# Mixing the last 64 tokens of two batches as two column tiles of the array

## Chip, cores, metric

The kernel runs on one core of one Trainium2 chip. The metric is the device time of one execution in microseconds (us). All runs quoted below were in the fast state (a program on one core has no second die to compare, so this rests on the spread of its own runs), and the granted TensorE clock of the profiled runs of before and after was 0.997 and 0.999. "Chunk" means 128 rows (tokens) of 512 values. PE is TensorE, DVE VectorE, ACT ScalarE, POOL GpSimd, SP SyncE, whose queue (SPq) starts most of the transfers that matter here.

## The reference

```python
# q, k, v: 8 batches x 8 heads x 576 tokens x 64;  x: 8 x 576 x 512
k_p = k.reshape(B, H, 72, 8, D).mean(axis=3)          # v_p likewise
attn = softmax(q @ k_p.T / 8)                         # 576 x 72 per head
x = (attn @ v_p).transpose(0, 2, 1, 3).reshape(B, S, H * D)
a1 = alpha1 * x + beta1
u = x + lam * np.einsum('ts,bsd->btd', w_tok, a1)     # token mix, 576 x 576
a2 = alpha2 * u + beta2
out = u + lam * (np.maximum(a2 @ w_ch1, 0.0) @ w_ch2) # 512 -> 2048 -> 512
```

576 tokens are four chunks of 128 and a remainder of 64. The remainders of two neighbouring batches share one chunk for everything after the token mix.

## The kernel before

The channel part runs in nine blocks of four chunks. Block n multiplies its chunks by both weight matrices and also prepares batch n+1: attention, token mix, transpose. A list of (place, function) pairs sets the order in which the pieces of a block are written into the program.

Every batch mixed its own five chunks, the fifth being the remainder. In `mix_T`, `c == 4` is the remainder; `xs` holds the scaled x of a batch, `wtT` the transposed weights. All 128 output rows were computed for it, and DVE read 64 of them: the upper half for an even batch, the lower half for an odd one.

```python
def att_AV(b, h):
    if "x" not in st:
        st["x"] = work.tile([P, 5, DM], FP, tag="x_tm", bufs=1, name="x_tm")
    ...
    nc.vector.tensor_tensor(out=x[:, :, dd:dd + D], in0=av[:, :, 0:64], in1=..., op=ALU.mult)

...
def mix_T(b, c, eng=nc.vector):
    key, s = chunk_of(b, c)                    # c == 4: the chunk (even b, 4), shared by two batches
    p0, p1 = (0, P) if c < 4 else (64 * (b % 2), 64 * (b % 2) + 64)
    xs = xs_pool[b % 2]
    ps_tok = gp("ps_tok")
    t0 = P * c - 64 * (b % 2) if c == 4 else P * c
    for sc in range(5):
        kk, at = (P, sc) if sc < 4 else (P, 5) if b % 2 else (65, 4)
        nc.tensor.matmul(out=ps_tok, lhsT=wtT[0:kk, at, t0:t0 + P],
                         rhs=xs[0:kk, sc, :], start=(sc == 0), stop=(sc == 4))
    nc.vector.tensor_tensor(out=s["u"][p0:p1, :], in0=st1[b]["x"][p0:p1, c, :],
                            in1=ps_tok[p0:p1, 0:DM], op=ALU.add)
    eng.tensor_tensor(out=s["u_bf"][p0:p1, :], in0=s["u"][p0:p1, :],
                      in1=al2_bc[p0:p1, :], op=ALU.mult)

def mix_uT(key):                               # u_bf -> u_fm, the operand of the channel part
    if key[0] > 1 or key == (0, 4):
        nc.sync.dma_start_transpose(out=u_fm[blk][...], in_=s["u_bf"])   # in SP's queue
        return
    ...                                        # otherwise a transpose on PE and a copy on ACT
```

SP's queue also carries the stores of results (`mlp_B`, when a chunk is finished) and the transposes of q for batch 2 (`att_F`, `att_Frem`). In the traces of before and after none of its 155 entries starts before the issue of the one ahead of it has ended, and an entry moved in the program moves in the queue (`rem_qT` from 85.36 to 77.51 us in the run with q first); this matters later.

The softmax here doesn't subtract the row's maximum and nothing guards it: scores larger than these inputs give would overflow.

## Time and profile before

| | before |
|---|---|
| time, 3 runs | 364.95 us (364.85 to 365.48) |
| span of the profiled run | 363.5 us |
| one matmul of 128 rows x 512 columns, in a dense stretch | 0.216 us |

The page and the stretches by stage are in the prediction. In the tiles' names, `ps_h` is the product of a block's chunks with `w_ch1`, `Hj` its maximum with 0 after a bias, made by ACT, `ps_ch` the product of `Hj` with `w_ch2`, `ps_tok` the token mix; `kpT` is the pooled k and `qT` and `rem_qT` the q of the attention, all transposed, `rem` standing for the last 64 tokens. What I compare later is the chain of waits in order of time: start, length, engine, tile and line, number of instructions. It is the best ruler for this kernel, because each piece on it starts when the one before allows it. First the group of the token mix (busy, mean ns of one, idle before and what ended it), then the chain. A matmul's record lasts 379 ns in the mean and the next starts 0.216 us after it, so the records overlap.

```profile
L518 PE MATMUL ps_tok<-xs,wtT 128*128 128x512 bf16 (+1 forms) x200 | 49.6, 379 | 1.8 <-DVE xs L484 1.8
```

```profile
65.44 1.25 PE ps_tok L518 x5
...
110.88 1.08 PE ps_tok L518 x5
...
118.01 4.32 PE ps_h L553 x20
...
155.06 4.32 PE ps_h L553 x20
...
303.26 13.81 PE ps_h L553 x64
```

The line at 110.88 is one of the four groups that the change takes out. 118.01, 155.06 and 303.26 are the first matmuls of blocks 2, 3 and 7. I use such starts as marks: the shift of a mark between two kernels is all that was won up to there.

### The profile page before, as it was taken

Reading aid. Unit: us, or ns where it says so; the run is one execution under the profiler, and the core shown is the slowest. Engines: PE = TensorE matmul, PEld = TensorE weight load, DVE = VectorE, ACT = ScalarE, POOL = GpSimd, SP = SyncE. Lnnn points to the kernel's source line nnn. Section 1 sums busy time; section 2 is a strip of 40 time slices with the busy share of each in tenths; the row PEclk is TensorE's granted clock in tenths of the full one; section 3 lists DMA queues with packets and bytes.
Section 4 is the critical chain, followed back from the end, with each engine's and each line's share of the span. In section 5 each row is a group of like instructions: output and inputs, shape, how many; then the busy total and the mean of one; then the engine's idle time right before and its main releaser. Section 6 shows DMA issues by size and latency. Waiting matters only on the chain.

```text
span 363.5 us, 5915 instructions
## 1 busy us (share of the span) xinstructions
PE 348.4 (96%) x2229; PEld 188.7 (52%) x2229; DVE 212.7 (59%) x456; ACT 153.9 (42%) x319; POOL 86.8 (24%) x99
## 2 busy tenths in 40 slices
PE   4888999899999999999999999999999999999994
PEld 1566666355644564456445644565456545545541
DVE  5574176669774878576857786677658761011011
ACT  2562995027800790069005910592049304703700
POOL 8469406252117000620053005300510000000000
PEclk9999999999999999999999999999999999999998
DMA  8999910998959872987198919872810032011012
GB/s 125 203 216 262 216 26 2 160 228 202 142 119 223 153 124 62 244 159 123 51 218 149 156 52 220 171 131 61 215 67 0 31 87 74 0 58 60 1 58 58
DMA packets 65886, 44.58 MB, mean 123 GB/s; under 512 B 32377, under 2 KB 57021, under 8 KB 65858
## 3 DMA queue, kind: packets, MB, share of 16 engines
q1 hardware_dynamic: 50480, 33.30, 38.3%
q0 software_dynamic: 15072, 10.76, 20.5%
q8 instruction: 17, 0.28, 0.3%
q10 hardware_dynamic: 306, 0.14, 0.2%
q14 instruction: 11, 0.09, 0.1%
HBM read 38.30 MB, written 9.44 MB: 131 GB/s over the span
## 4 chain that ended last, share of the span: by engine, by line
PE 90%; DVE 5%; ACT 1%; DMA 1%; issue 1%; ACTq 0%; DVEq 0%
PE ps_h L553 33%; PE ps_ch L571 33%; PE ps_tok L518 12%; PE ps_sc L450 4%; PE ps_av L469 2%; DVE x_tm L477 2%; PE ps_sc L453 1%; DMA vecs<-in_moe_alpha_dram 1%; PE ps_bc L278 1%; DVE kpT L416 1%; PE ps_kp L403 1%; DVE w L339 1%; PE ps_q L368 1%; DVE xs L484 0%; ACT u_fm L539 0%
## 5 line engine op out<-in xcount | busy, mean ns | idle before, releaser
L558 ACT ACTIVATE Hj<-ps_h,bias_cols 128x512 bf16<-128x512 f32 x144 | 98.7, 689 | 154.4 <-PE ps_h L553 153.5
L553 PE MATMUL ps_h<-u_fm,w 128*128 128x512 bf16 (+1 forms) x592 | 138.1, 374 | 1.3 <-ACT u_fm L539 1.1
L571 PE MATMUL ps_ch<-w,Hj 128*128 128x512 bf16 x576 | 134.2, 379 | 0.0
L571 PEld LDWEIGHTS <-Hj 128*128 128x128 bf16 x576 | 55.0, 98 | 62.0
L553 PEld LDWEIGHTS <-w 128*128 128x128 bf16 x592 | 63.4, 114 | 44.9 <-issue 1.8
L576 DVE TENSOR_TENSOR u_sb<-u_sb,ps_ch 128x512 f32<-128x512 f32 x36 | 24.7, 686 | 74.7 <-PE ps_ch L571 74.3
L518 PE MATMUL ps_tok<-xs,wtT 128*128 128x512 bf16 (+1 forms) x200 | 49.6, 379 | 1.8 <-DVE xs L484 1.8
L455 ACT ACTIVATE ET<-ps_sc 72x256 f16<-72x256 f32 (+1 forms) x128 | 44.5, 404 | 2.5 <-PE ps_sc L450 2.2
L520 DVE TENSOR_TENSOR u_sb<-x_tm,ps_tok 128x512 f32<-128x512 f32 (+1 forms) x40 | 27.5, 687 | 30.7 <-PE ps_tok L518 30.7
L477 DVE TENSOR_TENSOR x_tm<-ps_av,rec 128x320 f32<-128x320 f32 x64 | 31.4, 491 | 2.3
L147 POOL CAST rem_q<-rem_raw 128x256 bf16<-128x256 f32 x7 | 3.1, 437 | 123.3 <-DMA rem_raw<-in_q_dram 123.3
L518 PEld LDWEIGHTS <-wtT 128*128 128x128 bf16 (+1 forms) x200 | 19.2, 98 | 25.5 <-DVE xs L484 1.6
L522 DVE TENSOR_TENSOR u_bf<-u_sb,al_bc 128x512 bf16<-128x512 f32 (+1 forms) x38 | 29.0, 763 | 1.4
L438 DVE TENSOR_TENSOR v_u<-v_u 72x512 f32<-72x512 f32 (+1 forms) x48 | 28.3, 589 | 1.2
L450 PE MATMUL ps_sc<-qT,kpT 128*72 128x256 bf16 x128 | 25.4, 275 | 0.5 <-DVE kpT L416 0.4
L475 DVE RECIPROCAL rec<-ps_av 128x5 f32<-128x5 f32 x64 | 12.2, 191 | 18.6 <-PE ps_av L473 17.7
L469 PEld LDWEIGHTS <-ET 72*128 72x128 f16 x256 | 15.9, 98 | 11.9 <-issue 0.5
L162 POOL TENSOR_TENSOR k_raw<-k_raw 128x512 f32<-128x512 f32 x14 | 18.3, 1307 | 15.9 <-DMA k_raw<-in_k_dram 15.9
L164 POOL TENSOR_TENSOR k_bf<-k_raw 128x512 bf16<-128x512 f32 x14 | 19.4, 1386 | 1.1
L484 DVE TENSOR_TENSOR xs<-x_tm,lamal_bc 128x512 bf16<-128x512 f32 x26 | 18.3, 705 | 0.9
L469 PE MATMUL ps_av<-vp,ET 72*128 72x66 f16 x256 | 18.0, 193 | 0.3 <-ACT wtT L299 0.3
L416 DVE CAST kpT<-ps_kp 64x288 bf16<-64x288 f32 x26 | 11.8, 455 | 9.4 <-PE ps_kp L409 5.2
(111 smaller groups left out, 216.5 us busy)
## 6 DMA issues: line engine op xcount, KB each, us to landing
out_dram<-u_sb SPq DMA_DIRECT2D x32, 256.0 KB
k_raw<-in_k_dram SPq DMA_DIRECT2D x14, 512.0 KB
v_u<-in_v_dram SPq DMA_DIRECT2D x12, 512.0 KB
q_bf<-in_q_dram POOLq DMA_DIRECT2D x16, 256.0 KB, 6.7
w<-in_moe_w_ch_dram POOLq DMA_DIRECT2D x8, 512.0 KB, 10.9
v<-in_v_dram POOLq DMA_DIRECT2D x4, 256.0 KB, 6.8
out_dram<-u_sb SPq DMA_DIRECT2D x8, 128.0 KB
rem_raw<-in_q_dram SPq DMA_DIRECT2D x15, 64.0 KB
```

Source lines behind the costliest of these rows:

```text
L438: nc.vector.tensor_tensor(out=t[:, :, 0:n], in0=t[:, :, 0:n], in1=t[:, :, n:2 * n], op=ALU.add)
L450: nc.tensor.matmul(out=ps_sc[0:SPG, 0:256], lhsT=kpT_pool[u][:, half, h % 4, :], rhs=st["qT"][u][:, 2 * (h % 4):2 * (h % 4) + 2, :])
L455: nc.scalar.activation(out=ET[:, n0:n0 + n], in_=ps_sc[0:SPG, 0:n], func=AF.Exp, bias=0.0, scale=0.125)
L469: nc.tensor.matmul(out=av[:, c, :], lhsT=ET[:, m0:m0 + 128], rhs=vp1[:, hh, :])
L477: nc.vector.tensor_tensor(out=x[:, :, dd:dd + D], in0=av[:, :, 0:64], in1=rec.unsqueeze(2).to_broadcast((P, 5, D)), op=ALU.mult)
L518: nc.tensor.matmul(out=ps_tok, lhsT=wtT[0:kk, at, t0:t0 + P], rhs=xs[0:kk, sc, :], start=(sc == 0), stop=(sc == 4))
L520: nc.vector.tensor_tensor(out=s["u"][p0:p1, :], in0=st1[b]["x"][p0:p1, c, :], in1=ps_tok[p0:p1, 0:DM], op=ALU.add)
L522: eng.tensor_tensor(out=s["u_bf"][p0:p1, :], in0=s["u"][p0:p1, :], in1=al2_bc[p0:p1, :], op=ALU.mult)
L553: nc.tensor.matmul(out=ps_h[:, t0:t1], lhsT=w1_of(cc, j), rhs=u_fm[n][:, cc, t0:t1], start=(cc == 0), stop=(cc == 3))
L558: nc.scalar.activation(out=t, in_=ps_h, func=AF.Relu, bias=bias_cols[:, j:j + 1], scale=1.0)
L571: nc.tensor.matmul(out=ps, lhsT=Hj[n, j][:, 128 * m:128 * m + 128], rhs=w2[j // 4][:, j % 4, :], start=(j == 0), stop=(j == NJ - 1))
L576: nc.vector.tensor_tensor(out=u, in0=u, in1=ps, op=ALU.add)
```

## The change

The intent: the remainders of two batches, 64 output rows each, side by side in the array. In the trace after, such a matmul stands as a tile of 128*64, where one of 128 output rows stands as 128*128; in the built program the two of a pair sit at columns 0 and 64. The even batch's own mix goes away. The odd batch issues for each of the five accumulation steps one matmul for its partner into rows 0 to 63 of the accumulator and one for itself into rows 64 to 127. Since the partner's x must then live until the odd batch's mix, the two batches share a buffer of six sections: the even batch uses 1 to 5 with the remainder in 5, the odd one 0 to 4 with the remainder in 0. Sections 1 to 4 hold the full chunks of whichever batch came last.

```diff
 def att_AV(b, h):
-            st["x"] = work.tile([P, 5, DM], FP, tag="x_tm", bufs=1, name="x_tm")
+            st["x"] = st1[b - 1]["x"] if b % 2 else work.tile([P, 6, DM], FP, tag="x_tm", bufs=1, name="x_tm")
 ... (sections shifted by `odd` in the matmuls and in att_X)
-        nc.vector.tensor_tensor(out=x[:, :, dd:dd + D], in0=av[:, :, 0:64],
+        nc.vector.tensor_tensor(out=x[:, 1 - odd:6 - odd, dd:dd + D], in0=av[:, :, 0:64],
 def mix_T(b, c, eng=nc.vector):
-        p0, p1 = (0, P) if c < 4 else (64 * (b % 2), 64 * (b % 2) + 64)
+        parts = ((b % 2, 0, P),) if c < 4 else ((0, 0, 64), (1, 64, P))
         for sc in range(5):
-            ...
-            nc.tensor.matmul(out=ps_tok, lhsT=wtT[0:kk, at, t0:t0 + P],
-                             rhs=xs[0:kk, sc, :], start=(sc == 0), stop=(sc == 4))
+            for i, p0, p1 in parts:
+                kk, at = (P, sc) if sc < 4 else (P, 5) if i else (65, 4)
+                nc.tensor.matmul(out=ps_tok[p0:p1], lhsT=wtT[0:kk, at, P * c:P * c + p1 - p0],
+                                 rhs=xs_pool[i][0:kk, sc, :], start=(sc == 0), stop=(sc == 4))
+        for i, p0, p1 in parts:
+            ... (the add, once per part)
-        eng.tensor_tensor(out=s["u_bf"][p0:p1, :], in0=s["u"][p0:p1, :],
-                          in1=al2_bc[p0:p1, :], op=ALU.mult)
+        eng.tensor_tensor(out=s["u_bf"], in0=s["u"], in1=al2_bc, op=ALU.mult)
 # the order: mix_T(b, 4) only for odd b
-            todo.append((at, lambda c=c: mix_T(b, c)))
             if c < 4 or b % 2:
+                todo.append((at, lambda c=c: mix_T(b, c)))
-            todo.append((6.5, lambda: mix_T(0, 4)))          # block 0
```

More of the change, by code (lines that the diff above doesn't have):

```diff
@@ L466, in att_AV @@
         av = ps_av[:, 0:5 * 66].rearrange("p (c x) -> p c x", x=66)
+        odd = b % 2
         for c in range(4):
             m0 = 256 * (c % 2) + 128 * (c // 2)
-            nc.tensor.matmul(out=av[:, c, :], lhsT=ET[:, m0:m0 + 128],
+            nc.tensor.matmul(out=av[:, odd + c, :], lhsT=ET[:, m0:m0 + 128],
                              rhs=vp1[:, hh, :])
-        r0 = 512 - 64 * (b % 2)
-        nc.tensor.matmul(out=av[:, 4, :], lhsT=ET[:, r0:r0 + 128], rhs=vp1[:, hh, :])
+        r0 = 512 - 64 * odd
+        nc.tensor.matmul(out=av[:, 4 - 4 * odd, :], lhsT=ET[:, r0:r0 + 128], rhs=vp1[:, hh, :])
         rec = work.tile([P, 5], FP, tag="rec", bufs=2, name="rec")
@@ L484, in att_X @@
         eng.tensor_tensor(
-            out=xs[:, 0:4, cols], in0=x[:, 0:4, cols],
+            out=xs[:, 0:4, cols], in0=x[:, 1:5, cols],
             in1=lamal_bc[:, cols].unsqueeze(1).to_broadcast((P, 4, D * (h1 - h0))), op=ALU.mult)
         p0 = 64 * (b % 2)
-        eng.tensor_tensor(out=xs[p0:p0 + 64, 4, cols], in0=x[p0:p0 + 64, 4, cols],
+        eng.tensor_tensor(out=xs[p0:p0 + 64, 4, cols], in0=x[p0:p0 + 64, 5 - 5 * (b % 2), cols],
                           in1=lamal_bc[p0:p0 + 64, cols], op=ALU.mult)
@@ L511, in mix_T @@
         key, s = chunk_of(b, c)
-        p0, p1 = (0, P) if c < 4 else (64 * (b % 2), 64 * (b % 2) + 64)
-        xs = xs_pool[b % 2]
         ps_tok = gp("ps_tok")
-        t0 = P * c - 64 * (b % 2) if c == 4 else P * c
+        parts = ((b % 2, 0, P),) if c < 4 else ((0, 0, 64), (1, 64, P))
         for sc in range(5):
-            kk, at = (P, sc) if sc < 4 else (P, 5) if b % 2 else (65, 4)
-            nc.tensor.matmul(out=ps_tok, lhsT=wtT[0:kk, at, t0:t0 + P],
-                             rhs=xs[0:kk, sc, :], start=(sc == 0), stop=(sc == 4))
-        nc.vector.tensor_tensor(out=s["u"][p0:p1, :], in0=st1[b]["x"][p0:p1, c, :],
-                                in1=ps_tok[p0:p1, 0:DM], op=ALU.add)
-        eng.tensor_tensor(out=s["u_bf"][p0:p1, :], in0=s["u"][p0:p1, :],
-                          in1=al2_bc[p0:p1, :], op=ALU.mult)
+            for i, p0, p1 in parts:
[3 more added lines that the diff above has]
+        for i, p0, p1 in parts:
+            x = st1[b - b % 2 + i if c == 4 else b]["x"]
+            nc.vector.tensor_tensor(out=s["u"][p0:p1, :],
+                                    in0=x[p0:p1, 1 + c if c < 4 else 5 - 5 * i, :],
+                                    in1=ps_tok[p0:p1, 0:DM], op=ALU.add)
+        eng.tensor_tensor(out=s["u_bf"], in0=s["u"], in1=al2_bc, op=ALU.mult)
     def mix_uT(key):
```

## The prediction

> **What bounds the kernel now.** I read the page first: busy shares, the slices of the span, then the chain that ended last.
>
> ```profile
> span 363.5 us, 5915 instructions
> PE 348.4 (96%) x2229; PEld 188.7 (52%) x2229; DVE 212.7 (59%) x456; ACT 153.9 (42%) x319; POOL 86.8 (24%) x99
> PEclk9999999999999999999999999999999999999998
> PE 90%; DVE 5%; ACT 1%; DMA 1%; issue 1%; ACTq 0%; DVEq 0%
> PE ps_h L553 33%; PE ps_ch L571 33%; PE ps_tok L518 12%; PE ps_sc L450 4%; PE ps_av L469 2%; DVE x_tm L477 2%; PE ps_sc L453 1%; DMA vecs<-in_moe_alpha_dram 1%; PE ps_bc L278 1%; DVE kpT L416 1%; PE ps_kp L403 1%; DVE w L339 1%; PE ps_q L368 1%; DVE xs L484 0%; ACT u_fm L539 0%
> ```
>
> TensorE (PE) is 90% of the chain at full granted clock; the token mix, L518, is 12% of the span, 43.6 us. A busy PE can still hide short gaps, because matmul records overlap, so I asked for busy time by stage (stretches of 37 us from 81 us on; columns: stretch, length, then busy time and count of PE, PEld, DVE, ACT, POOL) and for PE's order around the last mix of an even batch.
>
> ```profile
> 81.00:118.00 37.00, 36.76 (x228) 19.52 (x227) 27.26 (x56) 15.49 (x32) 11.79 (x12) 1.00 0.80 171
> 118.00:155.00 37.00, 37.00 (x231) 19.84 (x229) 27.03 (x54) 15.35 (x32) 7.09 (x8) 1.00 0.67 145
> ...
> 109.85 1.03 PE L571 MATMUL ps_ch<-w,Hj 128*128 128x512 bf16 x4
> 110.72 1.24 PE L518 MATMUL ps_tok<-xs,wtT 128*128 128x512 bf16 x5
> 111.80 6.21 PE L571 MATMUL ps_ch<-w,Hj 128*128 128x512 bf16 x28
> 117.84 0.38 PE L553 MATMUL ps_h<-u_fm,w 128*128 128x512 bf16 x1
> ```
>
> The five of L518 hold PE from 110.72 to 111.80, 1.08 us, so 0.216 us each; the 28 after them take 117.84 - 111.80 = 6.04 us, again 0.216 us each. There is no gap: this part of the kernel is a queue on PE. From block 1 on (each of the nine blocks multiplies four 128-token chunks by both weight matrices; block n also prepares batch n+1), time taken from PE comes off the end; PE waits for others almost only before 66 us.
>
> [...] No 128x64 tile is in the trace before, so it cannot confirm the overlap; a mode change it does show, below. [...]
>
> **The change part by part.** Before, each batch mixed its last 64 tokens by itself: five matmuls of 128 output rows, of which DVE used 64. The change drops this for even batches and has the odd batch issue, per accumulation step, two matmuls of 64 output rows, one for each batch: columns 0-63, then 64-127. The built program confirms tile size 128x64 at column positions 0 and 64, 20 matmuls on each, and counts of instructions on PE that are the same before and after.
>
> *Removed from PE*: 4 groups x 5 x 0.216 = 4.32 us. Three stand in blocks 1, 3 and 5, where PE has no gap: 3 x 1.08 = 3.24 us. The first stands in block 0:
>
> ```profile
> 42.37 1.39 PE L518 MATMUL ps_tok<-xs,wtT 128*128 128x512 bf16 x5
> 43.59 1.03 PE L553 MATMUL ps_h<-u_fm,w 128*128 128x512 bf16 x4
> ...
> 44.66 0.69 ACT L558 ACTIVATE Hj<-ps_h,bias_cols 128x512 bf16<-128x512 f32 x1 [0.52 <-PE ps_h L553]
> ...
> 46.22 0.69 ACT L558 ACTIVATE Hj<-ps_h,bias_cols 128x512 bf16<-128x512 f32 x1 [0.55 <-PE ps_h L553]
> ```
>
> It holds PE 43.59 - 42.37 = 1.22 us. But from 46.22 to 54.6 ACT is busy without a break, and PE waits 0.23 us for its ET at 48.46. ACT can move forward only by the idle time it now spends on PE, 0.52 + 0.55 = 1.07 us. So I count 1.07, not 1.22. Sum removed: 4.31 us.
>
> *Kept on PE, if pairs overlap*: 5 pairs x 0.216 = 1.08 us where the odd batch's five stood: no difference.
>
> *Added*: four entries into and exits from 128x64 mode. The price comes from the only mode changes in this trace that stand in a dense stretch, 128 rows to 32 and back:
>
> ```profile
> 50.19 0.60 PE L426 MATMUL ps_v<-v,pool_v 128*72 128x256 f16 x4
> 50.72 0.40 PE L428 MATMUL ps_v<-v,pool_vr 32*72 32x256 f16 x2
> 51.05 0.41 PE L450 MATMUL ps_sc<-qT,kpT 128*72 128x256 bf16 x2
> 51.30 0.24 PE L453 MATMUL ps_sc<-rem_qT,kpT 128*72 128x64 bf16 x1
> ```
>
> One L426 record lasts 0.273 us and four merged 0.60, so the step is (0.60 - 0.273)/3 = 0.109 us. Without a mode change these eight matmuls of 256 columns would hold PE for 8 x 0.109 = 0.87 us; they hold it from 50.19 to 51.30, 1.11 us. One round trip costs 0.24 us. [...] With 0.03 us for the second tile's start (an estimate from the 33 ns between the one-column matmuls of L349), 4 x 0.27 = 1.08 us.
>
> *DVE*: the 64-row adds of L520 stay, 8 x 0.685 us. Eight 64-row casts of L522 at 0.836 us become four of 128 rows at 0.743: 6.7 - 3.0 = 3.7 us less on an engine 59% busy and waiting for PE in these stages. Beside PE: zero. The sixth section of x adds 2 KiB per partition and no instruction; L477 still writes 320 elements per partition.
>
> **Sum**: -4.31 + 1.08 = -3.2 us. 364.95 - 3.2 = 361.75; I say 361.8.
>
> **Rivals.** *The two tiles do not run side by side*[...]: then ten matmuls of 0.216 us per group, nothing saved, and 4 x 0.24 us added: 365.9. For: the trace shows no two PE matmuls of this shape closer than 0.216 us. [...] A half-way case, say 0.29 us a pair, costs 5 x 4 x 0.07 = 1.5 us: 363.3. *ACT or DVE bounds block 0* and gives nothing of its 1.07 us back: 362.8. For: PE waits 1.11 us for DVE's xs at 65.44. Against: DVE is itself paced by ps_av from PE there (0.60 us waits), so it moves along. *A new wait*: the pair's chunk is ready half a block to a block later. (0,4) was mixed at 43 us and will be at about 75; it is first multiplied in block 2, near 118 us. That leaves over 40 us; the DVE work after the mix grows from 0.69 + 0.84 to 2 x 0.69 + 0.74 us, 0.6 us more, a DMA transpose follows at 1.2 us of issue: hidden. *A shared x buffer* makes the next even batch wait for the odd one's last read. Before, with one buffer, every batch waited likewise; the first write of the next batch comes about 15 us after that read (112.0 to 127.8 across blocks 1 and 2): no wait. *DMA loads that were just in time*: POOL's sum of k ends near 114.5 us and PE uses it at about 122, so 1 us per block takes little of that slack.
>
> **Range and chances.** Full overlap with cheap to dearer switches spans 361.0 to 362.6; half overlap or a lost block 0 reaches 363.6. I give 361.0 to 363.6 for 8 in 10, the rest mostly to no overlap. Two per cent is 7.3 us, more than the whole 4.32 us that could go, so faster by over 2% has 0.01; slower by 2% (372.2) would need serial tiles and some 6 us of new waits: 0.01; within 2%: 0.98.
>
> **What would show it.** In the changed trace the pair's matmuls should start some 0.03 us or less apart with 0.216 us from pair to pair; each group should hold PE about 1.35 us, with some 0.1 us missing at its entry and at its exit. L518's place after four chunks of batches 2, 4, 6 should be empty, and blocks 1, 3, 5 shorter by 1.08 us, blocks 2, 4, 6 longer by 0.27. ACT should start the Hj of 46.22 near 45.15. Pairs 0.43 us apart make me wrong towards 366; an idle PE before ps_kp or ps_av in block 2 or later would mean a wait I did not see.

## The result, and the profile after

| | before | after |
|---|---|---|
| time, 4 runs each | 365.16 us | 361.85 us (361.39 to 362.13) |
| ratio | | 0.9908 (95%: 0.9891 to 0.9925) |
| span of the profiled run | 363.5 us | 360.4 us |
| DVE busy | 212.7 us | 209.5 us |

A ratio here is the mean time of one kernel's fast runs over that of the other's of the same rounds, so it is not quite the ratio of the medians beside it. By the mark of 2% the two are the same; the gain of 0.9% is outside the spread of the runs. The page after, its span, its chain by engine, and the group of the mix:

```profile
span 360.4 us, 5916 instructions
...
PE 89%; DVE 4%; ACT 3%; DMA 2%; SPq 1%; issue 1%; ACTq 0%; DVEq 0%
...
L518 PE MATMUL ps_tok<-xs,wtT 128*128 128x512 bf16 (+3 forms) x200 | 44.5, 380 | 1.8 <-DVE xs L485 1.8
```

L518 still has 200 matmuls, now in two more forms. PE is still the chain, but DMA has risen from 1% to 2% and SPq has appeared with 1%: the first sign of something new. ACT has risen from 1% to 3%: between 40 and 47 us the chain now runs over it, where before it ran over PE up to 46.22. One pair group among its neighbours, PE in order of time (start, length, group):

```profile
145.25 1.03 PE L573 MATMUL ps_ch<-w,Hj 128*128 128x512 bf16 x4
146.21 1.27 PE L518 MATMUL ps_tok<-xs,wtT 128*64 128x512 bf16 x10
147.41 6.22 PE L573 MATMUL ps_ch<-w,Hj 128*128 128x512 bf16 x28
```

The same view over a narrow window, cut so that only the last full matmul and the first pair are seen:

```profile
145.90 0.38 PE L573 MATMUL ps_ch<-w,Hj 128*128 128x512 bf16 x1
146.21 0.41 PE L518 MATMUL ps_tok<-xs,wtT 128*64 128x512 bf16 x2
```

Two records begin inside 146.21 to 146.62, where one alone lasts 0.38: the pair starts within a few nanoseconds (3 or 4 ns in the records, in all 20 pairs of the trace). The second pair starts 0.240 us after the first, the later ones 0.216 apart. So ten matmuls hold PE for 147.41 - 146.21 = 1.20 us. Between the start of the last L573 (145.90) and the first pair 0.31 us pass, where 0.216 is the usual step, and as much at the exit. Entry costs 0.093 us, the first pair 0.022, exit 0.096 and 0.011: one visit to the tiled mode costs about 0.22 to 0.23 us. By mode I mean the tile shape that the trace prints, 128*64 here and 128*128 around it; what PE does in that time, no trace shows. Both tiles of a pair write one PSUM tile, and the results are correct.

The chain of waits after, to be laid beside that of before:

```profile
64.32 1.25 PE ps_tok L518 x5
...
73.80 1.20 PE ps_tok L518 x10
...
116.34 4.32 PE ps_h L555 x20
...
153.63 4.32 PE ps_h L555 x20
...
300.13 13.81 PE ps_h L555 x64
```

The marks, shifts from before to after:

| mark (start of) | before | after | shift | predicted | what lies between |
|---|---|---|---|---|---|
| first mix of batch 1 | 65.44 | 64.32 | -1.12 | -1.07 | group of batch 0 gone |
| block 1, first ps_h | 80.53 | 79.64 | -0.89 | -0.80 | first pair group, one mode visit |
| block 1, first ps_ch | 98.47 | 97.88 | -0.59 | -0.80 | **nothing predicted: 0.30 lost** |
| block 2, first ps_h | 118.01 | 116.34 | -1.67 | -1.88 | group of batch 2 gone |
| block 3 | 155.06 | 153.63 | -1.43 | -1.61 | second pair group |
| block 4 | 192.11 | 189.58 | -2.53 | -2.69 | group of batch 4 gone |
| block 5 | 229.16 | 226.87 | -2.29 | -2.42 | third pair group |
| block 6 | 266.21 | 262.84 | -3.37 | -3.50 | group of batch 6 gone |
| block 7 | 303.26 | 300.13 | -3.13 | -3.23 | fourth pair group |

Each removed group gives 1.08 to 1.12 us and each pair group takes 0.23 or 0.24 back. One step was not foreseen, in block 1. There PE, and then SP's queue, show what it is (idle before an instruction and its releaser in brackets):

```profile
87.69 0.24 PE L453 MATMUL ps_sc<-rem_qT,kpT 128*72 128x64 bf16 x1 [0.57 <-DMA rem_qT<-rem_q]
```

PE waits for `rem_qT`, the transposed remainder of batch 2's q. The kernel before has another wait instead, 0.24 us for `kpT` one head later (at 89.31), and that one is gone after; 0.57 - 0.24 is the 0.3 lost. SP's queue before, then after (start, length of issue, line, kind, tile):

```profile
78.47 0.37 SPq L578 DMA_DIRECT2D out_dram<-u_sb  x1
...
85.03 1.28 SPq L381 DMA_TRANSPOSE rem_qT<-rem_q  x1
```

```profile
79.01 0.37 SPq L580 DMA_DIRECT2D out_dram<-u_sb  x1
79.43 1.33 SPq L534 DMA_TRANSPOSE u_fm<-u_bf  x1
...
85.36 1.19 SPq L381 DMA_TRANSPOSE rem_qT<-rem_q  x1
```

The first store of results starts 0.54 us later than before, and the transpose of q, which stands behind it and behind the shared chunk's own transpose (L534), 0.33 us later. Its user on PE comes 0.9 us earlier. A slack of about half a microsecond turned into a wait of about that size; in a second profiled run of the same kernel the wait was 0.34 us. Why the stores are late, DVE and POOL of the kernel after tell:

```profile
76.46 1.80 DVE L525 TENSOR_TENSOR u_bf<-u_sb,al_bc 128x512 bf16<-128x512 f32 x1
...
76.45 1.26 POOL L162 TENSOR_TENSOR k_raw<-k_raw 128x512 f32<-128x512 f32 x1 [0.56 <-DVE u_sb L522]
```

The cast of the shared chunk took 1.80 us where one alone takes 0.69: POOL's sum of k started 10 ns earlier and ended at 77.71. DVE's add that precedes the store stands behind the cast and starts at 78.30 (77.76 before). The cast ended at 78.26, 0.55 us after POOL's sum. In the rerun of this kernel (78.14 after 77.59) and in the run with q first (78.16 after 77.61) it was 0.55 us too. Had the cast done nothing until the sum ended, it would have ended at 77.71 + 0.69 = 78.40, an estimate 0.14 us too late; how the two shared that time is not shown.

### The profile page after: what moved, and what is told of

It reads as the page before. It is cut to its first block, busy times and chain, and to the rows that moved or that the text cites. A ratio compares the mean times of both kernels' runs of the same rounds, so it can differ in the third digit from the quotient of the medians.

```text
span 360.4 us, 5916 instructions
## 1 busy us (share of the span) xinstructions
PE 345.3 (96%) x2229; PEld 186.7 (52%) x2229; DVE 209.5 (58%) x452; ACT 154.1 (43%) x319; POOL 86.6 (24%) x99
## 4 chain that ended last, share of the span: by engine, by line
PE 89%; DVE 4%; ACT 3%; DMA 2%; SPq 1%; issue 1%; ACTq 0%; DVEq 0%
PE ps_ch L573 33%; PE ps_h L555 32%; PE ps_tok L518 11%; PE ps_sc L450 4%; PE ps_av L470 2%; DVE x_tm L478 2%; PE ps_sc L453 1%; ACT Hj L560 1%; DMA vecs<-in_moe_alpha_dram 1%; PE ps_bc L278 1%; PE ps_kp L403 1%; DMA rem_qT<-rem_q 1%; SPq L363 1%; DVE w L339 1%; PE ps_q L368 1%
## 5 line engine op out<-in xcount | busy, mean ns | idle before, releaser
L573 PE MATMUL ps_ch<-w,Hj 128*128 128x512 bf16 x576 | 133.7, 379 | 0.0
L573 PEld LDWEIGHTS <-Hj 128*128 128x128 bf16 x576 | 54.7, 98 | 62.7 <-issue 1.6
L518 PE MATMUL ps_tok<-xs,wtT 128*128 128x512 bf16 (+3 forms) x200 | 44.5, 380 | 1.8 <-DVE xs L485 1.8
L518 PEld LDWEIGHTS <-wtT 128*128 128x128 bf16 (+3 forms) x200 | 17.3, 100 | 23.6 <-issue 1.8
L438 DVE TENSOR_TENSOR v_u<-v_u 72x512 f32<-72x512 f32 (+1 forms) x48 | 27.5, 573 | 1.2
L525 DVE TENSOR_TENSOR u_bf<-u_sb,al_bc 128x512 bf16<-128x512 f32 x34 | 26.3, 775 | 1.2
```

What stands on the lines that cost most here:

```text
L438: nc.vector.tensor_tensor(out=t[:, :, 0:n], in0=t[:, :, 0:n], in1=t[:, :, n:2 * n], op=ALU.add)
L518: nc.tensor.matmul(out=ps_tok[p0:p1], lhsT=wtT[0:kk, at, P * c:P * c + p1 - p0], rhs=xs_pool[i][0:kk, sc, :], start=(sc == 0), stop=(sc == 4))
L525: eng.tensor_tensor(out=s["u_bf"], in0=s["u"], in1=al2_bc, op=ALU.mult)
L573: nc.tensor.matmul(out=ps, lhsT=Hj[n, j][:, 128 * m:128 * m + 128], rhs=w2[j // 4][:, j % 4, :], start=(j == 0), stop=(j == NJ - 1))
```

## The experiments

Ten kernels ran, in three jobs, all with correct results. The kernel before ran beside them and gave 364.85, 364.97 and 365.03 us. Each edit is against the kernel after. Besides the time I use the stretch from the first ps_h of block 2 to that of block 7, which holds the places of two removed groups (batches 4 and 6) and three pair groups (batches 3, 5 and 7), and none of the wait in block 1: 185.25 us before, 183.79 after.

### Does the move gain anything without the tiles?

```diff
+        ps = [ps_tok, gp("ps_tok")] if c == 4 else [ps_tok, ps_tok]
-                nc.tensor.matmul(out=ps_tok[p0:p1], lhsT=wtT[0:kk, at, P * c:P * c + p1 - p0],
+                t0 = P * c - 64 * i if c == 4 else P * c
+                nc.tensor.matmul(out=ps[i], lhsT=wtT[0:kk, at, t0:t0 + P],
 ... (the add reads ps[i])
```

> The x buffer of six sections, the late place of both last chunks and the single cast stay; but the ten matmuls of a group are of 128 output rows into two PSUM tiles, as in the kernel before, so no column tiling. Theory: a group holds PE 10 x 0.216 = 2.16 us and not 1.31 (1.08 and the mode change 0.23): 4 x 0.85 = 3.4 us more than the changed kernel, about 365.3, the time of the kernel before. Rival (the gain comes from moving the first mix out of the crowded start, from the buffer, or from the work that VectorE saves): stays near 361.9.

The two mixes stand together as in the change, but each with 128 output rows in an accumulator of its own. Measured: 364.90 us (12 runs), ratio to before 1.0003 (0.9995 to 1.0011). PE in order of time:

```profile
146.32 2.33 PE L520 MATMUL ps_tok<-xs,wtT 128*128 128x512 bf16 x10
148.48 1.24 PE L575 MATMUL ps_ch<-w,Hj 128*128 128x512 bf16 x5
```

Ten matmuls hold PE for 2.16 us, 10 x 0.216. The stretch is 186.37 us, 2.58 more than after, 0.86 per group: five matmuls more (1.08) less one mode visit (0.23) make 0.85. So the whole gain is that the tiles run side by side, and moving the work is worth nothing by itself.

### What does a pair cost, and what a mode visit?

The first of two edits issues every pair group twice over (the second pass starts afresh, so the result holds):

```diff
-        for sc in range(5):
+        for sc in list(range(5)) * (1 if c < 4 else 2):
```

> Each group's five pairs are computed twice, the second time over the first, in one stay in the mode; the result is unchanged. Theory (a pair costs what one full matmul costs, and the mode change is paid once a group): 4 x 5 x 0.216 = 4.3 us more than the changed kernel, about 366.2 us, with 2.28 us from the first start to the start of the next full matmul. Rival (a pair costs more in a longer run, the loads of weights falling behind, at 0.25 to 0.43 us): 366.9 to 370.5.

Measured: 365.79 us (11 runs), ratio 1.0027 (1.0019 to 1.0036). The stretch is 187.05 us, 3.26 more than after: 1.087 per group, 5 x 0.217. Five further pairs cost what five single matmuls cost. The price of a visit, 0.23 us, isn't paid again, so it belongs to the change of mode and not to the pairs.

The second edit cuts each pair group in two, with four ps_ch matmuls between:

```diff
-                todo.append((at, lambda c=c: mix_T(b, c)))
 ... (for c == 4; for c < 4 as before)
+                    todo.append((at, lambda c=c: mix_T(b, c, first=0, last=3)))
+                    todo.append((at + 0.9, lambda c=c: mix_T(b, c, first=3, last=5)))
```

> Each group of ten half-width matmuls is cut into six and four with four matmuls of 128x128 tiles between, so four more entries into and exits from the 128x64 mode and no other work. Theory: the mode change costs PE 0.23 us a round trip: 4 x 0.23 = 0.9 us more than the changed kernel, about 362.8 us, with about 0.1 us missing at each of eight entries and eight exits in the trace. Rival (the gaps seen at the group's edges are not the mode change, but a wait of the group's inputs or results, so they don't double): 361.9.

Measured: 363.18 us (6 runs, 362.64 to 364.17), ratio 0.9958 (0.9946 to 0.997). The stretch is 184.48 us, 0.69 more than after: 0.23 for each visit added. The two views agree on the price. The timed runs lost 1.3 us, where four visits make 0.9, and scattered more than those of after. The profiled run was the fastest of the six, and its mark at block 2 was not late (116.20), so that rest is open.

### Must the two tiles alternate?

```diff
-        for sc in range(5):
-            for i, p0, p1 in parts:
+        for i, p0, p1 in parts:
+            for sc in range(5):
```

> Same instructions as the changed kernel, but in each of the four groups the five matmuls of columns 0-63 stand first and the five of columns 64-127 after them, so neighbours lie in the same column tile but once. Theory (the gain is the overlap of two neighbours in different tiles, in order): nine steps of 0.216 us in place of five, a group holds PE 1.94 us and not 1.08, plus the same mode change: 4 x 0.86 = 3.5 us more than the changed kernel, about 365.3 us. Rival A (the engine overlaps matmuls of different tiles out of order, or a matmul of 64 columns is simply cheaper than one of 128): no change, about 361.9. Rival B (no overlap even at the seam): 366.2.

Now the five of one tile stand before the five of the other. If matmuls start strictly in program order, only the seam overlaps and nearly all is lost. Measured: 363.11 us (4 runs), ratio 0.9949 (0.9937 to 0.9962). PE in order of time, and then the same view narrowed to the group's end:

```profile
146.65 1.51 PE L518 MATMUL ps_tok<-xs,wtT 128*64 128x512 bf16 x10
148.09 1.25 PE L573 MATMUL ps_ch<-w,Hj 128*128 128x512 bf16 x5
```

```profile
147.54 0.62 PE L518 MATMUL ps_tok<-xs,wtT 65*64 65x512 bf16 x3
```

The group holds PE for 1.44 us, not the 2 or so of one tile after the other, and the stretch grows by 0.72, 0.24 per group: about one step of 0.216. The second line shows why. The matmul of 65 rows is the fifth in the program, the last of the first tile, and it is the head of the last three that start: it starts eighth. The sixth, first of the second tile, had started with the second, four places ahead of its turn. So PE started matmuls of the other tile before earlier ones of the first. Strict order, which forecast 365.3 us, fails, and so does the rival of no loss, 361.9. A look-ahead of about four is my estimate from this one run, and it makes a forecast for longer runs: with n matmuls per tile, the first n - 4 run alone, then four pairs, then n - 4 alone, 2n - 4 steps. For ten that is 16 steps instead of 10:

```diff
+        for i, p0, p1 in parts:
+            for sc in list(range(5)) * (1 if c < 4 else 2):
```

> Each group's pairs computed twice as in the run of doubled pairs, but the ten matmuls of columns 0-63 stand first and the ten of columns 64-127 after them. In the run of five and five, the sixth matmul in the program started with the second, four ahead of its turn. Theory W (the engine looks a fixed number of instructions ahead): here the eleventh can't start before about the seventh, so a group takes 16 or 17 steps of 0.216 us and not the 10 of alternating pairs: 4 x 1.3 to 1.5 us = 5 to 6 us over the run of doubled pairs, 371 to 372 us. Theory Q (each column tile has a queue that doesn't wait for the other): the eleventh starts with the second, 11 steps, about 1 us over it: 366.8. Strict order in the program would give 19 steps: 373.6.

Measured: 371.66 us (4 runs), ratio 1.018 (1.0165 to 1.0194).

```profile
148.61 3.68 PE L518 MATMUL ps_tok<-xs,wtT 128*64 128x512 bf16 x20
152.22 0.60 PE L573 MATMUL ps_ch<-w,Hj 128*128 128x512 bf16 x2
```

The twenty hold PE for 3.61 us. Sixteen steps make 3.46, and the ten of the kernel after also held PE 0.12 longer than their five steps. In the records the eleventh, first of the second tile, starts with the seventh, again four places ahead of its turn. Against the same twenty in alternation the stretch grows by 191.00 - 187.05 = 3.95 us, 1.32 per group, 6 x 0.22. In both runs the second tile began four places ahead, and alternation in the program is what makes the pairs whole: 2.28 us for the twenty in alternation (146.59 to 148.87 in the doubled pairs), 3.61 us for ten and ten. What holds it at four is open.

### What is the new wait, and what would it take to remove it?

The kernel after was run again beside these, unchanged:

> The changed kernel again, unedited, on the same chip as the three runs beside it, so that small differences are read against it. Expected ratio to the kernel before 0.991, with the wait of PE for rem_qT of 0.3 to 0.6 us near 87 us in its trace.

It gave 361.84 us (361.60 to 362.09), with a stretch of 183.79, so the marks repeat.

First I put the suspected transfer behind those that it delays: the transpose of the shared chunk moves from block 0 to a place after batch 2's q.

```diff
+            todo.append((0.9, lambda: mix_uT((0, 4))))                 # list of batch 2
-                todo.append((at + 1.8, lambda key=key: mix_uT(key)))
+                if key != (0, 4):
+                    todo.append((at + 1.8, lambda key=key: mix_uT(key)))
```

> The changed kernel, but the DMA transpose of the shared chunk of batches 0 and 1 is issued after the transposes of batch 2's q and of rem_q, not before them in SyncE's queue. Theory (the wait of 0.57 us of PE for rem_qT near 87 us comes from that queue: the chunk is cast later than before, the transpose waits for it, and those behind it wait too): the wait for rem_qT is gone; PE may wait 0.2 us for kpT there, as in the kernel before, so 0.3 to 0.57 us less than the changed kernel. Rival (rem_qT is late because of its own input, the cast on GpSimd, or of the DMA engines): the wait stays.

Measured: 361.38 us (4 runs, 361.20 to 361.72), ratio 0.9902 (0.9889 to 0.9915). SP's queue, then DVE and POOL:

```profile
77.95 2.83 SPq L580 DMA_DIRECT2D out_dram<-u_sb  x4
80.89 2.77 SPq L363 DMA_TRANSPOSE qT<-q_bf  x2
83.76 1.19 SPq L381 DMA_TRANSPOSE rem_qT<-rem_q  x1
...
76.51 0.69 DVE L525 TENSOR_TENSOR u_bf<-u_sb,al_bc 128x512 bf16<-128x512 f32 x1
...
76.54 1.80 POOL L162 TENSOR_TENSOR k_raw<-k_raw 128x512 f32<-128x512 f32 x1 [0.54 <-DVE u_sb L522]
```

`rem_qT` is issued 1.6 us earlier, PE's wait for it is gone, and block 2 starts at 115.75 instead of 116.27 (the rerun): 0.5 us. Here DVE's cast started 30 ns before POOL's sum, and it is POOL that took 1.80 us, where its sum takes 1.26 alone: it ended at 78.34, 1.14 us after the cast (77.20). So in these two runs the one that started second was the one held up, and this edit changed two things at once. It also shows that the collision made the first store late, and not the second add on DVE: with that add but a cast of 0.69 us the store is issued at 77.95, before the 78.47 of the kernel before. It has the lowest median of all versions, 0.46 us below the rerun of after, but the intervals of the ratio overlap; the trace says 0.5, the times alone do not settle it.

To part queue from cast, I lengthened the cast on purpose, in two halves of 64 rows:

```diff
-        eng.tensor_tensor(out=s["u_bf"], in0=s["u"], in1=al2_bc, op=ALU.mult)
+        for _, p0, p1 in parts:
+            eng.tensor_tensor(out=s["u_bf"][p0:p1, :], in0=s["u"][p0:p1, :],
+                              in1=al2_bc[p0:p1, :], op=ALU.mult)
```

> The changed kernel, but the cast and scaling of the shared chunk is done in two halves of 64 rows again, so VectorE gets back the 4 instructions of about 0.75 us that the change saved it. Theory (VectorE's saving lies beside PE's work): no change in blocks 2 to 8; at most the wait for rem_qT near 87 us grows by some tenths, because the transposes in SyncE's queue stand behind this cast: 361.9 to 362.4. Rival (the saved VectorE time is part of the gain): 4 x 0.75 = 3 us more, 364.9.

Measured: 363.59 us (18 runs, 362.6 to 365.9), ratio 0.9971 (0.9954 to 0.9987). DVE, then PE's wait:

```profile
76.80 3.32 DVE L526 TENSOR_TENSOR u_bf<-u_sb,al_bc 64x512 bf16<-64x512 f32 x2
...
89.58 0.24 PE L453 MATMUL ps_sc<-rem_qT,kpT 128*72 128x64 bf16 x1 [1.24 <-DMA rem_qT<-rem_q]
```

Two halves took 3.32 us beside POOL, where two unhindered ones would take some 1.4 (an estimate: twice the 0.69 of an unhindered cast). `rem_qT` was issued at 87.23, 1.9 us after the 85.36 of the kernel after, and block 2 began at 118.22, 1.9 us later. From there on nothing is lost: the stretch is 183.80. PE's waits here are the 1.24 us shown and 0.73 us just before, which the profile puts down to ACT's `Hj`. The median is over the 361.9 to 362.4 that was expected: in the profiled run the two halves (76.80 to 80.12) ran beside two POOL instructions, the sum of k from 76.64 to 77.90 and its cast from 77.98 to 79.57, and again ended 0.55 us after the second. That answers two questions. Longer DVE work in blocks 2 to 6 costs nothing, so DVE's saving there is worth nothing; and in block 0 it is not hidden. Why the runs scatter over 3.3 us, I did not settle; a different order of DVE and POOL from run to run would fit, but a profile shows one run only.

Next, the queue alone: batch 2's q goes first, well before the stores.

```diff
-        if b == 2:
-            todo.append((-2.0, lambda: cast_rem(b, nc.gpsimd)))
-            todo.append((-1.1, lambda: att_F(b, 0)))
-            ... (att_F(b, 2), att_Frem(b))
+        if first:
+            todo.append((27.6, lambda: cast_rem(2, nc.gpsimd)))
+            ... (att_F(2, 0), att_F(2, 2), att_Frem(2))
```

> The changed kernel, but batch 2's two q transposes and its rem_q transpose stand in SyncE's queue before block 0's first store of results and before the shared chunk's transpose, so none of them waits for VectorE any more. Theory (PE's wait for rem_qT comes from this queue behind VectorE): no wait for rem_qT, the time of the run with the transpose later or a little less, 361.2 to 361.4. Rival: the early transposes hold back the stores or the loads of v and cost as much elsewhere: 361.8.

Measured: 361.63 us (4 runs, 361.34 to 361.94), ratio 0.9906 (0.989 to 0.9923). This is the clean test: the cast is as long as in the rerun of after (1.49 us here, 1.52 there) and the first store as late (78.90 and 78.89), but `rem_qT` is issued at 77.51, PE's wait is gone, and the last ps_ch group of block 1 starts at 108.91 in place of 109.36 (the rerun): 0.45 us won in the trace. The timed runs show 0.2 us less than after, again inside the intervals, and between the forecast (361.2 to 361.4) and its rival (361.8); the trace decides here, not the times.

Last, both edits together, the long cast and q first:

> The run with the cast in halves (363.6, not the 361.9 to 362.4 that was expected) with the same three transposes moved ahead. Theory (the halves cost 1.7 us because VectorE, held up beside GpSimd's sums of k, delays SyncE's queue and with it rem_qT; nothing else in the kernel waits for it): the 1.2 us of waiting for rem_qT go, 362.4 or, if the wait of 0.7 us for ACT that stood before it goes as well, 361.4 to 361.7. Rival (the time on VectorE itself is on PE's path, through kpT or the free PSUM tiles): stays at 363 to 363.6.

Measured: 362.06 us (4 runs, 361.93 to 362.46), ratio 0.9919 (0.9904 to 0.9934). The two halves still took 3.38 us, `rem_qT` was issued at 77.41, and what is left on PE is this:

```profile
88.53 0.30 PE L450 MATMUL ps_sc<-qT,kpT 128*72 128x256 bf16 x1 [0.50 <-DVE kpT L416]
```

With q first, the long cast costs 362.06 - 361.63 = 0.4 us; with q behind it, 363.59 - 361.84 = 1.75 us. So most of the harm went through the queue. The rest agrees with the 0.50 us for `kpT`, which DVE itself makes after the cast; the forecast that nothing else waits for the cast (361.4 to 361.7 at best) missed this. The 1.75 is a difference of medians, one of them from runs that scatter over 3.3 us.

## Why the prediction was right, and where it was off

The time (361.85 against 361.8, range 361.0 to 363.6) and the class were right. By its own steps:

- **Removed from PE.** Right in size and in kind. Block 0 gave 1.12 us (predicted 1.07), and ACT's Hj of 46.22 started at 45.06 (predicted near 45.15). In the kernel after, the chain runs over ACT from 40 to 47.28 us without a break, so ACT does bound that stretch; the gain lies between its 1.07 us of idle time and the 1.22 for which the group held PE. The three later groups gave 1.08 to 1.10 us each (predicted 1.08).
- **Pairs run side by side.** Right, though beforehand it was an estimate of mine: no tile of 128*64 is in the trace before. The rival of serial tiles is refuted by the 3 or 4 ns between the two starts, and the move without tiles shows what it would have left: 364.90.
- **Cost of the mode.** That the column mode costs what the row mode of the kernel before does was an assumption of mine, and it held: 0.22 to 0.24 us for 64 columns and back, against 0.24 for 32 rows and back. Only the term for the second tile's start, taken from the wrong place at 0.03, was too large: the partner starts 3 or 4 ns later, and the first pair loses 0.022 us once. By the marks the four visits sum to 0.23 + 3 x 0.24 = 0.95 us, where 1.08 was predicted.
- **"Hidden", for the work after the mix.** This step failed. I asked how long the shared chunk's own reader in block 2 could wait (over 40 us) and not what stands behind the cast and behind the transpose in their queues. DVE's cast met POOL's sum of k, the stores came 0.5 us late, `rem_qT` 0.33 us, and PE lost 0.30 us in block 1. Three experiments show that the queue is the way: q first takes the wait away with the cast as long as before, the transpose last takes it away too (there the cast was short as well), and a longer cast lengthens it.
- **The sum.** Removed 1.12 + 1.08 + 1.10 + 1.08 = 4.38, mode visits 0.95, new wait 0.30: 3.13 us, as the last mark has it. The predicted 3.23 came close because 0.07 too little was removed and the visits were 0.13 too dear, while the wait of 0.30 was missing: errors that partly cancelled. That the time came within 0.05 us of the forecast is luck besides, since the forecast started from 364.95 and the runs of before beside the result gave 365.16.
- **Weight loads.** They are no term of the sum. In the kernel before a load took 98 ns for `Hj` and 114 ns for `w`, both with 128 columns, and 113 ns for `pool_v` with 72; in the kernel after, for the same `wtT` on L518, 98 ns with 128 columns and 109 ns with 64. They hid behind the matmuls either way: the step was 0.216 us with `Hj`, with `w` and from pair to pair.
- **DVE.** Its busy time fell by 3.2 us where 3.7 was predicted; the shift is worth zero beside PE, as said, which the cast in halves shows for blocks 2 to 6.
- **Shared x buffer, loads just in time.** No new wait on them is on the chain of waits from block 2 on.

## What to carry to other kernels

Here two independent products with 64 output rows each shared the array for the price of one: 0.216 us a pair, with 128 rows and 512 columns of data, plus 0.23 us for each visit to the mode. A group of ten took 1.31 us with its visit in place of 2.16, 1.65 times the speed. So gather the pairs in as few groups as can be and let the tiles alternate in the program. When work moves, look not only at who reads its result, but also at what is queued behind it on every engine and transfer queue: here a cast of 1.1 us too many reached PE through a queue of stores and transposes of unrelated data. A wait of half a microsecond is best proven with the marks of the chain, since the times of a few runs do not resolve it.
